# Top-32 attention with a gated mixer: the mask's biases made on ScalarE, and another order of the folds

## The chip, the cores and the metric

The kernel runs on one core of one Trainium2 chip. The metric is the device time of one execution in microseconds (us). Before the change the median of three runs is 985.09 us (983.68 to 985.43). The engines are named as the profile names them: PE is TensorE (matmuls), PEld its weight loads, DVE is VectorE, ACT is ScalarE, POOL is GpSimd, SP issues the DMAs.

## The reference

Three blocks follow one another, in float32, on batch 4, 8 heads, sequence 576, head width 64 (model width 512):

```
scores = q @ k.T / 8                       # per batch and head, 576 x 576
kth    = 32nd largest score of each row
attn   = softmax(where(scores >= kth, scores, -1e9)) @ v
x      = concat of the heads               # 4 x 576 x 512
gate   = sigmoid(causal 5-tap convolution of x along the sequence)
x      = (gate * (x @ w_val)) @ w_out
u      = x + token mixing (576 -> 256, relu, 256 -> 576)
out    = u + relu(u @ w_ch1) @ w_ch2       # 512 -> 1536 -> 512
```

## The kernel before

**Tiling.** Attention is cut into 80 units: 16 pairs of heads, each with four units of two 128-row tiles (one per head, `w = 2`) and a fifth of one tile that holds the last 64 rows of both heads (`w = 1`). A batch has 20 units. When a batch's units are done, its gate, its projections and its mixing follow: matmuls into the PSUM tiles `mo`, most of them as three products of split operands (L527 to L529).

**One unit** (`attn`). PE multiplies q with the left 288 columns of k into the PSUM tile `Sp` (L318), ACT copies them to `S` in SBUF (L324; L340 for `w = 1`), PE overwrites `Sp` with the right 288 columns, and ACT copies these to `S` too. Before its search for the 32 largest, DVE folds the row (`fold`, L412): left and right halves are compared element by element, the left half read from `S` and the right one straight from `Sp`. There are five folds. Called here by the names that the trace gives their outputs, they are: `A` (larger of the first quarters), `Sp` (larger of the second quarters, written beside the scores into columns 288 to 431 of the PSUM tile `Sp`), `y<-S,Sp` (all smaller ones), `X<-A,Sp` and `y<-A,Sp` (larger and smaller of the first two results). `topk` and `top32` then take eight at a time with MAX8 (L425 to L427, L442) and MATCH_REPLACE8 (L444), into `top`, 32 sorted values a row.

**The mask.** L346 makes two numbers per row in `nb`: the largest score times -0.125 and the 32nd times 2^100. It is one DVE instruction. Its two factors stand in the last two columns (1022 and 1023) of the PSUM tile `PT`, written once in `setup`. ACT makes `W` = relu(2^100 x (32nd - score)) with the second number as bias (L358), POOL subtracts `W` from `S` into `E` (L360), and ACT takes the exponential with the first number as bias (L363).

**Products with v.** PE transposes `E` into columns 0 to 639 of `PT` (L372), ACT copies them to `pT` (L377), PE multiplies with v into columns 640 to 767 of `PT` (L385 to L389), and ACT copies the result out (L393).

**What sets the order.** The kernel collects all operations with an engine, a cost, and keys that they read and write (class `Order`), places them by list scheduling with those costs, and issues them in order of planned start. Each engine then works through its list in order. The keys serve the planning only: the waits on semaphores are added afterwards from the tiles that the instructions touch, and accesses of two engines to the same PSUM bank come to wait for each other. For the planning, `fold` reads the key `Sp` in the first three folds alone, and the second copy of `Sp` writes that key, so it is placed behind these three. L346 has no key of `PT`.

**Buffers.** `S` has four, `top` and `nb` three, `E`, `W` and `pT` two each; `Sp` and `PT` have one each, of two PSUM banks.

Of the kernel before, what the change touches and what calls it, by code (L numbers as in the profile page):

```python
# [11 lines left out]
AF = mybir.ActivationFunctionType  # L12
OP = mybir.AluOpType
# [4 lines left out]
BIG = 2.0 ** 100  # L18
# [147 lines left out]
class Builder:  # L166
# [56 lines left out]
    def setup(self):  # L223
        nc = self.nc
        jp = self.tf[0][:, 0:128].bitcast(I32)
        nc.gpsimd.iota(jp, pattern=[[1, 128]], base=0, channel_multiplier=-1)
        nc.vector.tensor_scalar(self.ident, jp, 0.0, None, op0=OP.is_equal)
        z = self.tf[1][:, 0:64]
        nc.vector.memset(z, 0.0)
        for i in range(4):  # L230
            nc.vector.tensor_copy(self.rhl[:, i], z)
        for i in range(4):
            nc.vector.memset(self.xf[i][:, 0:4], 0.0)
        for i in range(self.nE):
            nc.vector.memset(self.Et[i][:, S:640], 0.0)
        nc.vector.memset(self.bad, 0.0)
        nc.vector.memset(self.PT[:, 1022:1023], -0.125)
        nc.vector.memset(self.PT[:, 1023:1024], BIG)


    def pe(self, c, f, r, w, late=0.0, part=1.0):
# [55 lines left out]
    def attn(self, p, u):  # L297

        nc = self.nc
        b, c = divmod(p, 4)  # L300
        i = self.cnt["unit"]
        self.cnt["unit"] += 1
        s = self.slot[p]
        w = 2 if u < 4 else 1
        St, kS = self.St[i % self.nS], [("S", i % self.nS, t) for t in range(w)]
        q, k = self.qk2[s][:, 0], self.qk2[s][:, 1]
        R = [("qk", s, 0), ("qk", s, 1)]
        Sp = self.Sp
        m, kM = self.top[i % 3], [("m", i % 3, t) for t in range(w)]
        if u < 4:  # L310

            for n in range(2):
                c0 = 288 * n

                def qk(c0=c0):
                    for t in range(2):
                        r = slice(64 * t, 64 * t + 64)
                        nc.tensor.matmul(Sp[:, t, 0:288], q[r, 128 * u:128 * u + 128], k[r, c0:c0 + 288],  # L318
                                         start=True, stop=True)

                self.pe(0.686, qk, R, ["Sp"])
                if n and self.fast:
                    self.fold(i, w, St, Sp[:, :, 0:288], kS)
                self.act(S, lambda c0=c0: nc.scalar.activation(St[:, :, c0:c0 + 288], Sp[:, :, 0:288], AF.Copy),  # L324
                         ["Sp"], [(x, n) for x in kS] + ["Sp"] * n)
        else:

            def qk():
                for c0, c1 in ((0, 288), (288, 512), (512, 576)):
                    n, s0 = divmod(c0, 288)  # L330
                    if c1 < S:
                        e = 288 if n == 0 else S
                        nc.tensor.matmul(Sp[0:64, n, 0:288], q[0:64, 512:S], k[0:64, c0:e], start=True, stop=True)
                    y = (c0 + 64) % S
                    nc.tensor.matmul(Sp[64:128, n, s0:s0 + c1 - c0], q[64:128, 512:S], k[64:128, y:y + c1 - c0],
                                     start=True, stop=True)

            self.pe(1.125, qk, R, ["Sp"])
            for n in range(2):
                self.act(288, lambda n=n: nc.scalar.activation(St[:, 0, 288 * n:288 * n + 288], Sp[:, n, 0:288], AF.Copy),  # L340
                         ["Sp"], [(kS[0], n)] + ["Sp"] * n)
                if n == 0 and self.fast:
                    self.fold(i, w, St, Sp[:, 1:2, 0:288], kS)
        nb, kN = self.nb[i % 3], ("nb", i % 3)
        (self.topk if self.fast else self.topk_any)(i, w, St, m, kS, kM)
        self.dve(2 * w, lambda: nc.vector.tensor_tensor(  # L346
            nb[:, 0:w], m[:, 0:w, 0:32:31], self.PT[:, 1022:1024].unsqueeze(1).to_broadcast([128, w, 2]), op=OP.mult), kM, [kN])
        vt = self.vt[s]
        o = self.PT[:, 640:768]
        pts = []  # L350
        E2, kE2 = self.Et[i % self.nE], [("E", i % self.nE, t) for t in range(2)]
        for t in range(w):
            j = self.cnt["tile"]
            self.cnt["tile"] += 1
            x, kx = St[:, t], [(kS[t], 0), (kS[t], 1)]
            E, W = E2[:, t * S:(t + 1) * S], self.Wt[j % self.nW]
            kE, kW = kE2[t], ("W", j % self.nW)
            self.act(S, lambda W=W, x=x, t=t: nc.scalar.activation(W, x, AF.Relu, bias=nb[:, t, 1:2], scale=-BIG),  # L358
                     kx + [kN], [kW], True)
            self.pool(S, lambda W=W, x=x, E=E: nc.gpsimd.tensor_tensor(E, x, W, op=OP.subtract),  # L360
                      kx + [kW], [kE])
            d = self.den[b % 2][:, c, 2 * u + t:2 * u + t + 1]
            self.act(S + 110, lambda E=E, d=d, t=t: nc.scalar.activation(  # L363
                E, E, AF.Exp, bias=nb[:, t, 0:1], scale=0.125, accum_out=d),
                [kE, kN], [kE, ("den", b % 2, c, 2 * u + t)], True)

            pT, kP = self.pT[j % self.nP], ("pT", j % self.nP)
            z = [0, 1, 2, 3, 4] if w == 1 else [5, 6, 7, 8, 4] if t else [0, 1, 2, 3]

            def tr(z=z):  # L370
                for y, k in enumerate(z):
                    nc.tensor.transpose(self.PT[:, y * 128:(y + 1) * 128], E2[:, k * 128:(k + 1) * 128], self.ident)  # L372

            n = 128 * len(z)
            kp = ["PT", "o"][:1 + (n > 512)]
            self.pe(0.109 * len(z) - 0.081, tr, kE2[0:1] if w == 2 and t == 0 else kE2, kp, 0.1)
            self.act(n, lambda pT=pT, n=n: nc.scalar.activation(pT[:, 0:n], self.PT[:, 0:n], AF.Copy), kp, [kP])  # L377
            pts.append((pT, kP))
        a, e = pts[0][0], pts[-1][0]
        n = 128 if w == 2 else 64  # L380
        g = 128 - n

        def pv():
            for y in range(4):
                nc.tensor.matmul(o[0:64, 0:n], vt[:, y], a[:, y * 128:y * 128 + n], start=(y == 0), stop=False)  # L385
                nc.tensor.matmul(o[64:128, 0:n], vt[:, 5 + y], e[:, y * 128 + g:y * 128 + 128], start=(y == 0), stop=False)
            r = slice(64, 128) if w == 2 else slice(0, 64)
            nc.tensor.matmul(o[0:64, 0:n], vt[0:64, 4], e[0:64, 512:512 + n], start=False, stop=True)
            nc.tensor.matmul(o[64:128, 0:n], vt[r, 4 if w == 2 else 9], e[r, 512 + g:640], start=False, stop=True)  # L389

        self.pe(1.39 if w == 2 else 0.877, pv, [x[1] for x in pts] + [("v", s)],
                ["o"], 0.1, 0.88)
        self.act(n, lambda: nc.scalar.activation(self.xf[c][:, 4 + 128 * u:4 + 128 * u + n], o[:, 0:n], AF.Copy),  # L393
                 ["o"], [("x", c, u)])

    def fold(self, i, w, St, right, kS):

        v = self.nc.vector  # L400
        kx = [(x, 0) for x in kS]
        A, Bm = self.At[:, 0:w], self.yt[:, 1].rearrange("p (t k) -> p t k", t=2)[:, 0:w]
        Ar = self.Sp[:, 0:w, 288:432]
        A1, A2 = self.Xt[i % 2][:, 0:w, 0:144], self.yt[:, 0].rearrange("p (t k) -> p t k", t=2)[:, 0:w, 0:144]
        kA, kB, kX = ([(n, t) for t in range(w)] for n in ("A", "B", ("X", i % 2)))
        l = St[:, 0:w, 0:288]
        kl, kr = kx + ["Sp"], ["Al", "Ar"]
        for o, ko, a, b, ka, f in ((A, ["Al"], l[:, :, 0:144], right[:, :, 0:144], kl, OP.max),
                                   (Ar, ["Ar"], l[:, :, 144:288], right[:, :, 144:288], kl, OP.max),
                                   (Bm, kB, l, right, kl, OP.min),  # L410
                                   (A1, kX, A, Ar, kr, OP.max), (A2, kA, A, Ar, kr, OP.min)):
            self.dve(w * a.shape[-1], lambda o=o, a=a, b=b, f=f: v.tensor_tensor(o, a, b, op=f), ka, ko)  # L412

# [381 lines left out]
```

## Time and profile before

| what | value |
|---|---|
| median of three runs | 985.09 us |
| the profiled execution, its own time | 985.71 us |
| its span, first to last instruction | 983.9 us |
| mean granted TensorE clock | 0.951 |
| PE, DVE, ACT, POOL busy | 870.9, 768.2, 554.1, 422.7 us |

The span leaves 1.8 us of the execution's own time outside it. Busy time is the union of an engine's instructions. An idle time is given with what ended it. Since each engine works in the order of its list, an instruction that waits holds up all that stands behind it.

### The profile page before, as it was taken

How to read it: one execution, taken by the hardware profiler on the slowest of the kernel's cores; microseconds unless marked ns; L12 is line 12 of the kernel's file. 1: busy time of each engine (PE TensorE's matmuls, PEld its weight loads, DVE VectorE, ACT ScalarE, POOL GpSimd, SP SyncE). 2: the span in 40 equal slices, each digit the busy share in tenths (PEclk: the TensorE clock that was granted, in tenths of full speed). 3: DMA queues.
4: the chain of work that ended last, by engine and by line, in shares of the span. 5: the costliest groups of instructions: out<-in, count | busy, mean ns of one | idle time of the engine just before them, and what ended most of it. 6: DMA issues, size and time to landing. Idle time of an engine off the chain costs nothing.

```text
span 983.9 us, 18581 instructions
## 1 busy us (share of the span) xinstructions
PE 870.9 (89%) x6585; PEld 714.7 (73%) x6585; DVE 768.2 (78%) x2735; ACT 554.1 (56%) x1095; POOL 422.7 (43%) x395
## 2 busy tenths in 40 slices
PE   3479587899898998889999999999999999989996
PEld 1246354588687777667787888778788889878996
DVE  8998988989899998999689769896997866912222
ACT  4476766767675757666676545477676543522100
POOL 2344445778686877754253222354343121412000
PEclk9767869999999999999999999999999999999998
DMA  3101104334245454542112334433032235231442
GB/s 108 36 14 54 36 27 142 126 128 175 78 132 179 154 173 156 173 164 82 62 47 100 129 102 151 138 103 108 15 102 87 86 120 182 91 107 65 156 166 95
DMA packets 33734, 106.96 MB, mean 109 GB/s; under 512 B 3872, under 2 KB 4128, under 8 KB 33632
## 3 DMA queue, kind: packets, MB, share of 16 engines
q1 hardware_dynamic: 33632, 105.68, 32.2%
q8 instruction: 54, 0.88, 0.4%
q14 instruction: 48, 0.39, 0.1%
HBM read 84.17 MB, written 21.50 MB: 107 GB/s over the span
## 4 chain that ended last, share of the span: by engine, by line
PE 50%; DVE 31%; ACT 12%; issue 4%; POOL 1%; DMA 0%; DVEq 0%; ACTq 0%; SPq 0%
PE mo L527 10%; PE mo L528 9%; PE mo L529 9%; PE Sp L318 6%; PE PT L372 5%; PE PT L385 5%; DVE top L442 5%; DVE Z L444 4%; DVE y L412 4%; ACT S L324 3%; DVE f L614 3%; DVE X L425 2%; ACT W L358 2%; ACT pT L377 2%; ACT E L363 2%
## 5 line engine op out<-in xcount | busy, mean ns | idle before, releaser
L527 PE MATMUL mo<-r,ring 128*128 128x288 f32 x1024 | 317.2, 310 | 6.0 <-DVE xf L594 2.0
L528 PE MATMUL mo<-r,ring 128*128 128x288 f32 x1024 | 303.1, 296 | 2.7 <-DVE r L477 1.9
L529 PE MATMUL mo<-r,ring 128*128 128x288 f32 x1024 | 302.7, 296 | 1.0 <-POOL ring L462 0.9
L360 POOL TENSOR_TENSOR E<-S,W 128x576 f32<-128x576 f32 x144 | 207.0, 1450 | 94.1 <-ACT W L358 78.8
L527 PEld LDWEIGHTS mo<-r,ring 128*128 128x128 f32 x1024 | 192.9, 188 | 31.7 <-issue 19.2
L528 PEld LDWEIGHTS mo<-r,ring 128*128 128x128 f32 x1024 | 193.1, 189 | 4.6 <-DVE r L477 3.0
L529 PEld LDWEIGHTS mo<-r,ring 128*128 128x128 f32 x1024 | 192.9, 188 | 1.7 <-POOL ring L462 1.7
L358 ACT ACTIVATE W<-S,nb 128x576 f32<-128x576 f32 x144 | 107.0, 770 | 77.8 <-DVE nb L346 77.1
L318 PE MATMUL Sp<-qk 64*128 64x288 f32 x512 | 111.7, 513 | 40.8 <-ACT S L324 17.6
L442 DVE MAX8 top<-Z 128x8 f32<-128x168 f32 x432 | 125.9, 323 | 0.7
L363 ACT ACTIVATE E<-E,nb 128x576 f32<-128x576 f32 x144 | 111.3, 773 | 24.9 <-POOL E L360 24.1
L372 PE MATMUL PT<-ident,E 128*128 128x128 f32 x656 | 107.4, 294 | 19.0 <-ACT pT L377 7.3
L377 ACT ACTIVATE pT<-PT 128x512 f32<-128x512 f32 (+1 forms) x144 | 94.2, 654 | 49.1 <-PE PT L372 48.3
L324 ACT ACTIVATE S<-Sp 128x576 f32<-128x576 f32 x128 | 83.2, 650 | 66.0 <-PE Sp L318 31.3
L431 POOL TENSOR_TENSOR bad<-X,top 128x6 f32<-128x6 f32 (+1 forms) x80 | 18.5, 231 | 224.6 <-DVE top L442 182.4
L372 PEld LDWEIGHTS PT<-ident,E 128*128 128x128 f32 x656 | 78.0, 148 | 48.1 <-ACT pT L377 14.6
L385 PE MATMUL PT<-pT,v 128*64 128x128 f32 (+1 forms) x640 | 86.6, 282 | 16.2 <-ACT pT L377 11.0
L318 PEld LDWEIGHTS Sp<-qk 64*128 64x128 f32 x512 | 44.7, 208 | 71.5 <-ACT S L324 29.9
L468 ACT ACTIVATE r<-mo 128x576 fp32r<-128x576 f32 (+2 forms) x76 | 47.3, 629 | 85.2 <-PE mo L529 80.7
L385 PEld LDWEIGHTS PT<-pT,v 128*64 128x64 f32 x640 | 67.8, 145 | 37.1 <-ACT pT L377 20.4
L636 DVE TENSOR_TENSOR f<-mo,f 128x576 f32<-128x576 f32 x64 | 47.9, 748 | 55.1 <-PE mo L529 55.1
L444 DVE MATCH_REPLACE8 Z<-top,Z 128x168 f32<-128x168 f32 x288 | 89.7, 317 | 0.0
(106 smaller groups left out, 1609.5 us busy)
## 6 DMA issues: line engine op xcount, KB each, us to landing
ring<-ch1d SPq DMA_DIRECT2D x36, 512.0 KB, 3.3
ring<-ch2d SPq DMA_DIRECT2D x36, 512.0 KB, 3.3
stage<-in_w_ch_dram SPq DMA_DIRECT2D x24, 512.0 KB, 3.6
qk<-in_qk_dram SPq DMA_DIRECT2D x32, 288.0 KB, 3.1
ch1d<-ring SPq DMA_DIRECT2D x12, 512.0 KB, 2.9
ch2d<-ring SPq DMA_DIRECT2D x12, 512.0 KB, 3.6
ring<-vald SPq DMA_DIRECT2D x12, 512.0 KB, 3.5
ring<-outd SPq DMA_DIRECT2D x12, 512.0 KB, 3.4
```

The source lines that it names most:

```text
L318: nc.tensor.matmul(Sp[:, t, 0:288], q[r, 128 * u:128 * u + 128], k[r, c0:c0 + 288], start=True, stop=True)
L358: self.act(S, lambda W=W, x=x, t=t: nc.scalar.activation(W, x, AF.Relu, bias=nb[:, t, 1:2], scale=-BIG), kx + [kN], [kW], True)
L360: self.pool(S, lambda W=W, x=x, E=E: nc.gpsimd.tensor_tensor(E, x, W, op=OP.subtract), kx + [kW], [kE])
L363: self.act(S + 110, lambda E=E, d=d, t=t: nc.scalar.activation(E, E, AF.Exp, bias=nb[:, t, 0:1], scale=0.125, accum_out=d), [kE, kN], [kE, ...
L372: nc.tensor.transpose(self.PT[:, y * 128:(y + 1) * 128], E2[:, k * 128:(k + 1) * 128], self.ident)
L377: self.act(n, lambda pT=pT, n=n: nc.scalar.activation(pT[:, 0:n], self.PT[:, 0:n], AF.Copy), kp, [kP])
L385: nc.tensor.matmul(o[0:64, 0:n], vt[:, y], a[:, y * 128:y * 128 + n], start=(y == 0), stop=False)
L442: self.dve(n, lambda src=src, o=o: v.max(o, src), k, [(kM, q)] + [kM] * (q in (0, 3)))
L444: self.repl(n, lambda src=src, o=o: v.match_replace(out=z, in_to_replace=o, in_values=src, imm_value=NEG), k + [(kM, q)], [kz])
L527: nc.tensor.matmul(o, wh, xh, start=(x == 0), stop=False)
L528: nc.tensor.matmul(o, wh, xl, start=False, stop=False)
L529: nc.tensor.matmul(o, wl, xh, start=False, stop=(x == last))
```

## The change

The DVE instruction of L346 goes, and with it the two constants in `PT`. Two ACT instructions take its place, one for each number, with the factor as an immediate; both read `top` and write `nb` in SBUF. `W` is placed behind the second, the exponential behind the first.

In `fold` the third fold (`y<-S,Sp`) moves ahead of the second (`Sp`), which for the planning now also depends on it; and the last two folds read the key `Sp`, so that the copy of the right half is placed behind all five.

```diff
-        nc.vector.memset(self.PT[:, 1022:1023], -0.125)
-        nc.vector.memset(self.PT[:, 1023:1024], BIG)
...
-        self.dve(2 * w, lambda: nc.vector.tensor_tensor(
-            nb[:, 0:w], m[:, 0:w, 0:32:31], self.PT[:, 1022:1024].unsqueeze(1).to_broadcast([128, w, 2]), op=OP.mult), kM, [kN])
+        for x, (z, f) in enumerate(((0, -0.125), (31, BIG))):
+            self.act(2 * w, lambda x=x, z=z, f=f: nc.scalar.activation(nb[:, 0:w, x], m[:, 0:w, z], AF.Copy, scale=f),
+                     kM, [(kN, x)])
...
-                     kx + [kN], [kW], True)
+                     kx + [(kN, 1)], [kW], True)
...
-                [kE, kN], [kE, ("den", b % 2, c, 2 * u + t)], True)
+                [kE, (kN, 0)], [kE, ("den", b % 2, c, 2 * u + t)], True)
...
-        kl, kr = kx + ["Sp"], ["Al", "Ar"]
+        kl, kr = kx + ["Sp"], ["Al", "Ar", "Sp"]
         for o, ko, a, b, ka, f in ((A, ["Al"], l[:, :, 0:144], right[:, :, 0:144], kl, OP.max),
-                                   (Ar, ["Ar"], l[:, :, 144:288], right[:, :, 144:288], kl, OP.max),
                                    (Bm, kB, l, right, kl, OP.min),
+                                   (Ar, ["Ar"], l[:, :, 144:288], right[:, :, 144:288], kl + kB, OP.max),
                                    (A1, kX, A, Ar, kr, OP.max), (A2, kA, A, Ar, kr, OP.min)):
```

The planner places everything anew. On DVE, a unit's folds in the second pair of heads stood like this before (numbers behind names tell buffers apart; `waits` names the engines that the row waits for):

```order
L412 TENSOR_TENSOR A<-S_71,Sp 128x288 [waits PE_49,Activation_49]
L346 TENSOR_TENSOR nb_84<-top_81,PT 128x4 [waits DVE_49,Activation_49]
L412 TENSOR_TENSOR Sp<-S_71,Sp 128x2x144 [waits DVE_49]
L412 TENSOR_TENSOR y<-S_71,Sp 128x576 [waits DVE_49]
L412 TENSOR_TENSOR X_75<-A,Sp 128x2x144
L412 TENSOR_TENSOR y<-A,Sp 128x2x144 [waits Activation_49]
L425 MAX X_75<-y 128x8 [waits DVE_49,Pool_49]
```

The same unit now, on DVE (the lines of the changed kernel are one or two lower; L496 is a weight conversion that the planner put between):

```order
L411 TENSOR_TENSOR A<-S_71,Sp 128x288 [waits PE_49,Activation_49]
L411 TENSOR_TENSOR y<-S_71,Sp 128x576
L496 TENSOR_SCALAR wa_106<-stage_63 128x512 [waits DMAHW4_49,Pool_49]
L411 TENSOR_TENSOR Sp<-S_71,Sp 128x2x144 [waits DVE_49]
L424 MAX X_75<-y 128x8
L411 TENSOR_TENSOR X_75<-A,Sp 128x2x144 [waits DVE_49]
L411 TENSOR_TENSOR y<-A,Sp 128x2x144
```

`nb` has left DVE's list, one wait on DVE's own results has gone from the first three folds, a MAX8 stands between the third and the fourth, and none of the last two folds waits for ACT.

On ACT, the stretch from one `Sp` copy to the next around the mask of another unit stood like this before:

```order
L324 ACTIVATE S_71<-Sp 128x2x288 [waits DVE_49,PE_49]
L358 ACTIVATE W_88<-S_70,nb_84 128x576 [waits Activation_49]
L358 ACTIVATE W_87<-S_70,nb_84 128x576 [waits Activation_49]
L393 ACTIVATE xf_162<-PT 128x128 [waits PE_49]
L324 ACTIVATE S_72<-Sp 128x2x288 [waits DVE_49,PE_49]
```

The mask of the same unit now, on ACT (L460 are splits of other data, L392 is the copy out of `PT`):

```order
L322 ACTIVATE S_71<-Sp 128x2x288 [waits PE_49]
L460 ACTIVATE ring_166<-wa_106 128x512 [waits Pool_49]
L345 ACTIVATE nb_84<-top_81 128x2 [waits DVE_49]
L345 ACTIVATE nb_84<-top_81 128x2
L460 ACTIVATE rhl<-rcp 128x9 [waits DVE_49]
L357 ACTIVATE W_88<-S_70,nb_84 128x576 [waits Activation_49]
L392 ACTIVATE xf_162<-PT 128x128 [waits PE_49]
```

The two new instructions stand ahead of `W`; the first waits for DVE, and `W` waits for ACT's own result.

## Rows read from the trace of the kernel before

**Rows 1.** The page: busy time of each engine, share of span, instructions.
```profile
PE 870.9 (89%) x6585; PEld 714.7 (73%) x6585; DVE 768.2 (78%) x2735; ACT 554.1 (56%) x1095; POOL 422.7 (43%) x395
```

**Rows 2.** Stretches, us: length, each engine's busy time (instructions), clock, DMA, GB/s.
```profile
0.00:194.00 194.00, 133.51 (x849) 83.28 (x850) 171.25 (x720) 125.20 (x263) 87.95 (x99) 0.80 0.21 68
194.00:450.00 256.00, 232.08 (x1819) 192.03 (x1818) 233.42 (x796) 168.31 (x329) 185.50 (x157) 0.99 0.43 147
450.00:850.00 400.00, 385.00 (x3080) 325.61 (x3077) 325.40 (x1172) 238.07 (x469) 137.00 (x133) 1.00 0.31 101
850.00:984.00 134.00, 120.29 (x845) 113.80 (x843) 38.13 (x52) 22.52 (x35) 12.22 (x8) 0.97 0.36 120
```

**Rows 3.** DVE timeline, 98 to 118 us: start, length, instruction [idle before, ended by].
```profile
98.46 0.44 DVE L412 TENSOR_TENSOR A<-S,Sp 128x288 f32<-128x288 f32 x1
99.35 0.16 DVE L346 TENSOR_TENSOR nb<-top,PT 128x4 f32<-128x4 f32 x1 [0.45 <-ACT pT L377]
99.42 0.46 DVE L412 TENSOR_TENSOR Sp<-S,Sp 128x288 f32<-128x288 f32 x1
99.91 0.75 DVE L412 TENSOR_TENSOR y<-S,Sp 128x576 f32<-128x576 f32 x1
100.59 0.45 DVE L412 TENSOR_TENSOR X<-A,Sp 128x288 f32<-128x288 f32 x1
100.95 0.45 DVE L412 TENSOR_TENSOR y<-A,Sp 128x288 f32<-128x288 f32 x1
...
106.27 0.44 DVE L412 TENSOR_TENSOR A<-S,Sp 128x288 f32<-128x288 f32 x1
...
107.92 0.45 DVE L412 TENSOR_TENSOR X<-A,Sp 128x288 f32<-128x288 f32 x1
109.08 0.45 DVE L412 TENSOR_TENSOR y<-A,Sp 128x288 f32<-128x288 f32 x1 [0.72 <-ACT S L324]
...
114.61 0.45 DVE L412 TENSOR_TENSOR A<-S,Sp 128x288 f32<-128x288 f32 x1
```

**Rows 4.** Timeline of all engines, 199 to 200 us.
```profile
199.10 0.27 PE L389 MATMUL PT<-pT,v 64*64 64x128 f32 x1
...
199.47 0.16 DVE L346 TENSOR_TENSOR nb<-top,PT 128x4 f32<-128x4 f32 x1 [2.31 <-PE PT L389]
...
199.67 0.78 ACT L358 ACTIVATE W<-S,nb 128x576 f32<-128x576 f32 x1 [2.15 <-DVE nb L346]
```

**Rows 5.** DVE's L346 in 0:194, 194:450, 450:850: count | busy, mean ns | idle before.
```profile
L346 DVE TENSOR_TENSOR nb<-top,PT 128x4 f32<-128x4 f32 (+1 forms) x21 | 3.1, 154 | 11.6 <-PE PT L389 4.8 <-PE PT L372 3.5 <-ACT pT L377 1.9
...
L346 DVE TENSOR_TENSOR nb<-top,PT 128x4 f32<-128x4 f32 (+1 forms) x23 | 3.5, 153 | 11.1 <-PE PT L389 6.7 <-PE PT L372 2.4 <-issue 1.3
...
L346 DVE TENSOR_TENSOR nb<-top,PT 128x4 f32<-128x4 f32 (+1 forms) x36 | 5.5, 152 | 6.9 <-PE PT L389 5.1 <-ACT pT L377 1.1 <-PE PT L372 0.2
```

**Rows 6.** DVE's last folds: 0:194, then 194:450 (two), then 450:850.
```profile
L412 DVE TENSOR_TENSOR y<-A,Sp 128x288 f32<-128x288 f32 (+1 forms) x22 | 9.3, 423 | 5.9 <-ACT S L324 5.0 <-ACT S L340 1.0
...
L412 DVE TENSOR_TENSOR y<-A,Sp 128x288 f32<-128x288 f32 (+1 forms) x22 | 9.3, 421 | 4.2 <-ACT S L324 3.7 <-ACT S L340 0.5
L412 DVE TENSOR_TENSOR X<-A,Sp 128x288 f32<-128x288 f32 (+1 forms) x22 | 9.2, 419 | 2.4 <-ACT S L324 2.1 <-ACT S L340 0.2
...
L412 DVE TENSOR_TENSOR y<-A,Sp 128x288 f32<-128x288 f32 (+1 forms) x36 | 15.0, 418 | 10.9 <-ACT S L324 8.7 <-ACT S L340 1.4 <-PE Sp L318 0.6
```

**Rows 7.** ACT timeline, 72.5 to 75 us: a small copy and what follows.
```profile
72.65 0.20 ACT L461 ACTIVATE rhl<-rcp 128x9 fp32r<-128x9 f32 x1
72.75 0.58 ACT L377 ACTIVATE pT<-PT 128x512 f32<-128x512 f32 x1
```

**Rows 8.** In 0:194: ACT's copy of Sp, and DVE's first fold.
```profile
L324 ACT ACTIVATE S<-Sp 128x576 f32<-128x576 f32 x37 | 24.0, 650 | 24.6 <-PE Sp L318 9.1 <-DVE X L412 7.9 <-DVE y L412 6.5
...
L412 DVE TENSOR_TENSOR A<-S,Sp 128x288 f32<-128x288 f32 (+1 forms) x22 | 9.1, 412 | 1.0 <-ACT diag L601 1.0
```

**Rows 9.** PE's products with v in 0:194.
```profile
L385 PE MATMUL PT<-pT,v 128*64 128x128 f32 (+1 forms) x160 | 25.9, 318 | 12.9 <-ACT pT L377 8.2 <-DVE nb L346 4.6
```

**Rows 10.** Line L527's weight loads: ns min/median/max, first and last start us.
```profile
L527 PEld LDWEIGHTS mo<-r,ring x1024: 186/188/330, 193.8 to 974.8; 128*128 128x128 f32 x171
```

## The prediction

> **What bounds the kernel now.** The page's busy times come first: PE 870.9 us and DVE 768.2 us of a span of 983.9, ACT 56% [rows 1]. A mean like this mixes stages, so the second view is the busy time by stretches, cut where the mixer's matmuls begin (193.8 us [rows 10]) and where attention has ended. It shows four stages [rows 2]. From 0 to 194 us there is attention alone: DVE is busy 171.3 of 194 us (88%), PE 133.5, and PE's granted clock averages 0.80, between its levels of 1.2 and 2.4 GHz. From 194 to 450 DVE (233.4 of 256) and PE (232.1) are both at 91%. From 450 to 850 PE is at 96% (385.0 of 400) and DVE at 81%. From 850 on PE does the last batch's mixing nearly alone. So DVE sets the pace first, both share it next, then PE.
>
> The third view is DVE's timeline in the first stage. From one unit's first fold to the next it takes 7.81 us (98.46 to 106.27) and 8.34 us (106.27 to 114.61), and between them the list is dense but for two holes: `nb` waited 0.45 us for an ACT copy out of `PT`, and a last fold waited 0.72 us for ACT's copy of `Sp` [rows 3]. Neither hole is arithmetic: the fold and the copy both only read `Sp`, and `nb` reads two columns that nobody writes. A larger hole of this kind is at 199 us: the last matmul into `PT` ends at 199.37, `nb` starts at 199.47 after 2.31 us of waiting, and `W` on ACT follows at 199.67 [rows 4]. The fourth view, the groups by line, gives the holes their sum in each stage [rows 5, 6].
>
> **The change part by part.** The sums are made against the profiled execution, 985.71 us, of which 983.9 are its span; the median is 0.6 us lower.
>
> *Removal of `nb` from DVE.* It is busy 3.1, 3.5 and 5.5 us in the three stages at some 0.153 us each [rows 5], but neighbours overlap: the next fold starts 0.07 us after it [rows 3]. I take 0.1 us, between 0.07 and 0.15: 21, 23 and 36 instructions give 2.1, 2.3 and 3.6 us.
>
> *Its waits.* 11.6, 11.1 and 6.9 us of DVE idle [rows 5] go, since the new instructions touch only SBUF. PE waited for `nb` too, 4.6 us in its products with v in the first stage alone [rows 9], and that goes with them.
>
> *The fold's waits for the copy.* 5.9 us in the first stage, 4.2 + 2.4 = 6.6 in the second, 10.9 in the third (0.6 of these for PE) [rows 6]. In the new order the copy comes behind all folds, so none of them can wait for it.
>
> *The new order of folds.* Two folds that don't depend on each other start 0.36 us apart (100.59, 100.95); a fold that waits for the write before it starts 0.49 after it (99.42, 99.91) [rows 3]. Before, two of the first three folds wait so, now one. That is 0.13 us per unit: 2.7, 3.0 and 4.7 us. Between zero (another wait takes its place) and twice that, I take it once. The MAX8 put ahead of the fourth fold covers that one's wait: it takes the 0.36 us or so that the write needs.
>
> *The two instructions on ACT.* No row shows them. The nearest is a copy of 9 columns: 0.20 us, and the next instruction begins 0.10 us after it starts [rows 7]. As `W` waits for the second of them, a pair holds ACT between 0.20 us (two issues) and 0.40 us (both in full); I take 0.10 + 0.20 = 0.30. In the first stage that is 21 x 0.30 = 6.3 us on an engine with 194 - 125.2 = 68.8 us free [rows 2], so its busy time is hidden; what isn't hidden is the way from the last `top` to `W`, 0.1 to 0.2 us longer than the 0.20 from the start of `nb` to `W` [rows 4]. Four buffers of `S` lie behind that way, and I cost it at nothing. If that cover is gone, it costs up to 44 x 0.30 = 13.2 us before 450 us.
>
> *The later copy.* It now waits for the fifth fold. Before, ACT's copy already waited for a `y` or an `X` fold (6.5 and 7.9 us in the first stage), so much of the delay is there today [rows 8]. At most the copy moves by two folds of 0.36 us. While `Sp` is refilled, DVE has the unit's whole search ahead (106.27 to 114.61 less the folds, over 5 us [rows 3]); that hides it. DVE's first fold waited 1.0 us in the stage, for something else [rows 8].
>
> *The sum.* First stage: instruction and fold order give 2.1 + 2.7 = 4.8 us in full, as DVE sets the pace; the waits of 11.6 + 5.9 = 17.5 us I count by half, 8.8, because what a hole absorbs today (a late `Sp`, a late `S`) will partly be waited for elsewhere. That is 13.6. Second stage: 2.3 + 3.0 + 11.1 + 6.6 = 23.0, PE's own idle time of 23.9 us allows it, but PE is as full as DVE, so a third: 7.7. Third stage: PE's 15.0 us of idle time cap everything; I take 1, since DVE is not what PE waits for there. Last stage: nothing. 985.7 - 13.6 - 7.7 - 1 = 963.4, less the 0.6 of the median 962.8; I give 963 us. With only the instructions and the order counted in the first stage, and half of them in the second, the sum ends at 985.7 - 4.8 - 2.7 = 978; with all of the first two stages at 985.7 - 22.3 - 22 = 941.
>
> **The rivals.**
>
> *Everything comes through.* The holes close and nothing takes their place in the first two stages: about 941 to 950, 945 in the middle. For it: the dense units of 7.8 to 8.3 us, in which DVE never waits for data except at these two places. Against it: PE would have to run from 194 to 450 us without any hole.
>
> *The waits move.* The copy now always comes last, `Sp` is refilled later, and DVE waits at its first fold what it doesn't wait at its last: only instructions and fold order are left, 978 us (973 to 983). For it: PE's clock is low in the first stage, so a refill is slow. Against it: the 5 us of search.
>
> *Nothing arrives.* The gain of the first stage is spent in the second, where the newly placed list meets a full PE: 985 us, within the bound below.
>
> *Slower.* The pair stands at the head of ACT's list and waits for DVE's `top`; behind it stand the copies of `Sp` and `PT`, which DVE and PE wait for. Before, `nb` waited on DVE, and `W` alone waited on ACT. If each of the 44 pairs before 450 us holds the copies up by its full 0.30 us and the holes saved on DVE come back as waits for `S` and `Sp`, the sum is 985.7 + 13.2 = 999 us. It decides once DVE's waits at the first fold exceed the 17.5 us saved in the first stage, from 1.0 now. For it: the list of ACT, where a split and a copy out of `PT` now stand among pair and `W`. Against it: ACT's 68.8 us free. The Trainium skill ("ScalarE: Activation LUTs", Rules for kernel authors) speaks for this rival: it sends multiplications to VectorE rather than ScalarE. Going by that page's 186 ns + 0.833 ns per element for an instruction with immediates, a pair would be an estimated 0.38 us against DVE's one of 0.153, and the 999 would become about 1002; the trace's 0.20 us for 9 columns agrees with that price [rows 7], and whether the rule holds here is a matter of which engine sets the pace.
>
> **How the numbers follow.** Forecast 0.50 (own range 952 to 973), everything through 0.13, waits move 0.18, nothing arrives 0.07, slower 0.12. A measurement of this kernel can tell about 0.2%, 2 us, from no change. Faster is 0.50 + 0.13 + 0.18 = 0.81, the same 0.07, slower 0.12. The range of 943 to 986 leaves out the slower case and some 0.05 of the lowest.
>
> **What would show it.** Right: `nb` absent from DVE; the last folds without idle time before them; a first stage so much shorter that the first L527 matmul comes near 180 us instead of 193.8; a DVE share over 91% in the first stage; ACT's pair at 0.2 us an instruction and no growth of the wait of PE for ACT's copies. Wrong: the first fold's idle time up by several us in the first stage (the waits moved), ACT's copies starting later after their data is there (slower), or the first stage shorter by 10 us with the total unmoved (nothing arrives).

## The result, and the profile after

The changed kernel takes 953.55 us in the median of four runs (951.91 to 954.19). Against runs of the kernel before on the same chip the ratio is 0.967, with a 95% interval of 0.963 to 0.970; measured once more on another chip it is 0.970 (0.967 to 0.973). That is 3.0 to 3.3% less; the forecast was 963, with a range of 943 to 986. The profiled execution took 951.91 us, of which 950.0 are its span. Ratios here are of undisturbed runs alone.

The page of the changed kernel, busy time of each engine (against [rows 1]):

```profile
PE 859.5 (90%) x6585; PEld 710.5 (75%) x6585; DVE 764.7 (80%) x2653; ACT 572.5 (60%) x1255; POOL 426.9 (45%) x395
```

DVE has 82 instructions fewer (80 `nb` and two constants), ACT 160 more. PE does the same 6585 matmuls in 11.4 us less; the stretches below put 10.5 of these into the first stage, where its granted clock has risen (11 of its matmuls also lie in another stretch now). The mixer's first matmuls, in the changed kernel (against [rows 10]):

```profile
L526 PEld LDWEIGHTS mo<-r,ring x1024: 186/188/330, 178.4 to 940.9; 128*128 128x128 f32 x171
```

So the first stage ends 15.4 us earlier. To compare the rest, both spans are cut at the same three events: the first of these matmuls, the issue of batch 0's last output, and that of batch 2's. The outputs, issued by SP, first before, then after:

```profile
423.80 0.38 SPq L710 DMA_DIRECT2D out_dram<-f  x1
...
835.14 0.34 SPq L710 DMA_DIRECT2D out_dram<-f  x1
```

```profile
385.53 0.42 SPq L709 DMA_DIRECT2D out_dram<-f  x1
...
801.11 0.34 SPq L709 DMA_DIRECT2D out_dram<-f  x1
```

Busy times in the stretches between these events (columns as in [rows 2]), before:

```profile
0.00:193.80 193.80, 133.31 (x848) 83.08 (x848) 171.05 (x718) 125.13 (x263) 87.75 (x99) 0.80 0.21 67
193.80:423.80 230.00, 210.09 (x1644) 173.77 (x1642) 208.98 (x730) 151.98 (x299) 175.47 (x148) 0.99 0.45 152
423.80:835.10 411.30, 393.65 (x3142) 332.74 (x3144) 338.18 (x1227) 246.29 (x482) 140.69 (x137) 1.00 0.31 102
835.10:984.00 148.90, 133.83 (x958) 125.13 (x954) 49.98 (x62) 30.69 (x52) 18.75 (x12) 0.96 0.35 114
```

And after:

```profile
0.00:178.40 178.40, 122.81 (x837) 77.61 (x837) 166.65 (x679) 124.69 (x294) 89.10 (x97) 0.89 0.24 80
178.40:385.50 207.10, 198.44 (x1561) 167.39 (x1561) 195.01 (x643) 147.40 (x318) 170.23 (x142) 1.00 0.47 162
385.50:801.10 415.60, 405.37 (x3242) 341.56 (x3237) 353.05 (x1271) 269.70 (x593) 148.81 (x145) 0.99 0.32 102
801.10:950.00 148.90, 132.83 (x958) 123.97 (x954) 49.98 (x62) 30.69 (x52) 18.73 (x12) 0.97 0.34 114
```

In the first stretch DVE's idle time falls from 193.8 - 171.1 = 22.7 to 178.4 - 166.7 = 11.7 us, and its busy time by 4.4: that is the 15.4. The work in the two first stretches isn't quite the same: the shorter one holds the folds of 21 units instead of 22 and the search of 38 tiles instead of 40, and in exchange more weight conversions (L496, L499 and L501, 24.6 us against 18.3 before). The second stretch is 22.9 us shorter. But PE did 83 matmuls less in it, 11.7 us, and these turn up in the third: what the second really gained is PE's idle time, from 19.9 to 8.7, 11.2 us. In the third PE's idle time falls from 17.7 to 10.2, 7.4 us, although the stretch with its added work is 4.3 longer. The last doesn't move. 15.4 + 11.2 + 7.4 = 34.0, against 33.9 for the span.

DVE's folds in the first stretch of the changed kernel (against [rows 6, 8]):

```profile
L411 DVE TENSOR_TENSOR y<-S,Sp 128x576 f32<-128x576 f32 (+1 forms) x21 | 14.3, 680 | 2.4 <-PE Sp L316 2.3
L411 DVE TENSOR_TENSOR Sp<-S,Sp 128x288 f32<-128x288 f32 (+1 forms) x21 | 9.0, 428 | 0.4
L411 DVE TENSOR_TENSOR A<-S,Sp 128x288 f32<-128x288 f32 (+1 forms) x21 | 8.8, 417 | 2.8 <-PE Sp L316 2.8
L411 DVE TENSOR_TENSOR y<-A,Sp 128x288 f32<-128x288 f32 (+1 forms) x21 | 8.7, 416 | 0.0
L411 DVE TENSOR_TENSOR X<-A,Sp 128x288 f32<-128x288 f32 (+1 forms) x21 | 8.5, 407 | 0.0
```

The last folds no longer wait. Whichever fold comes first (`A` in some units, `y<-S,Sp` in others) now waits for PE's refill of `Sp`, 5.1 us in all, against 1.0 for `A` before, which was a wait for ACT.

The mask in the changed kernel, ACT and DVE from 102.4 to 104 us (against [rows 3, 4]), and a second pair on ACT:

```profile
102.48 0.30 ACT L345 ACTIVATE nb<-top 128x2 f32<-128x2 f32 x2 [1.64 <-DVE top L441]
102.48 0.69 DVE L411 TENSOR_TENSOR y<-S,Sp 128x576 f32<-128x576 f32 x1
...
102.68 0.20 ACT L460 ACTIVATE rhl<-rcp 128x9 fp32r<-128x9 f32 x1
102.78 0.76 ACT L357 ACTIVATE W<-S,nb 128x576 f32<-128x576 f32 x1
103.09 0.44 DVE L411 TENSOR_TENSOR A<-S,Sp 128x288 f32<-128x288 f32 x1
...
103.56 0.46 DVE L411 TENSOR_TENSOR Sp<-S,Sp 128x288 f32<-128x288 f32 x1
...
103.94 0.46 DVE L424 MAX8 X<-y 128x8 f32<-128x288 f32 x1
```

```profile
74.78 0.29 ACT L345 ACTIVATE nb<-top 128x2 f32<-128x2 f32 x2
75.01 0.78 ACT L357 ACTIVATE W<-S,nb 128x576 f32<-128x576 f32 x1
```

The pair keeps ACT busy for 0.30 us. In the first place a small instruction for other data (`rhl`) stands between it and `W`; in the second `W` follows directly and starts 0.23 us after the pair does. DVE goes on with its folds beside it.

### The profile page after: what moved, and what is told of

It reads as the page before. It is cut to its first block, busy times and chain, and to the rows that moved or that the text cites. A ratio compares the mean times of both kernels' runs of the same rounds, so it can differ in the third digit from the quotient of the medians.

```text
span 950.0 us, 18427 instructions
## 1 busy us (share of the span) xinstructions
PE 859.5 (90%) x6585; PEld 710.5 (75%) x6585; DVE 764.7 (80%) x2653; ACT 572.5 (60%) x1255; POOL 426.9 (45%) x395
## 4 chain that ended last, share of the span: by engine, by line
PE 62%; DVE 25%; ACT 7%; POOL 2%; issue 2%; DMA 2%; SPq 0%; DVEq 0%; ACTq 0%; POOLq 0%
PE mo L526 14%; PE mo L527 13%; PE mo L528 13%; PE Sp L316 6%; PE PT L371 5%; PE PT L384 4%; DVE top L441 4%; DVE Z L443 4%; DVE y L411 3%; DVE f L613 2%; DVE X L424 2%; PE PT L387 2%; PE mo L605 2%; DVE wa L501 1%; ACT r L467 1%
## 5 line engine op out<-in xcount | busy, mean ns | idle before, releaser
L527 PE MATMUL mo<-r,ring 128*128 128x288 f32 x1024 | 303.0, 296 | 2.8 <-POOL r L461 2.2
L526 PEld LDWEIGHTS mo<-r,ring 128*128 128x128 f32 x1024 | 192.9, 188 | 32.6 <-issue 19.9
L527 PEld LDWEIGHTS mo<-r,ring 128*128 128x128 f32 x1024 | 193.1, 189 | 4.8 <-POOL r L461 3.4
L316 PE MATMUL Sp<-qk 64*128 64x288 f32 x512 | 106.3, 493 | 25.8 <-ACT S L322 18.3
L371 PE MATMUL PT<-ident,E 128*128 128x128 f32 x656 | 105.1, 290 | 23.8 <-ACT E L362 13.4
L430 POOL TENSOR_TENSOR bad<-X,top 128x6 f32<-128x6 f32 (+1 forms) x80 | 20.9, 261 | 230.5 <-DVE top L441 224.0
L371 PEld LDWEIGHTS PT<-ident,E 128*128 128x128 f32 x656 | 77.5, 146 | 50.2 <-ACT E L362 19.9
L384 PE MATMUL PT<-pT,v 128*64 128x128 f32 (+1 forms) x640 | 87.3, 284 | 9.2 <-ACT pT L376 9.1
L385 PE MATMUL PT<-pT,v 128*64 128x128 f32 (+1 forms) x640 | 87.4, 284 | 0.0
```

What stands on the lines that cost most here:

```text
L526: nc.tensor.matmul(o, wh, xh, start=(x == 0), stop=False)
L527: nc.tensor.matmul(o, wh, xl, start=False, stop=False)
```

## The experiments

Theories: **waits**, that VectorE's holes at `nb` and at the folds set the pace and that closing them is the gain; against it that only one half of the change does anything, that `nb` had to leave VectorE, or that the new **plan** as such is what helps. The table gives the ratio to the kernel before with its 95% interval, the ratio times 985.3 us (the absolute medians come from several chips), and two events of the one profiled execution: first L527-type matmul, and batch 0's last output.

| kernel | ratio | interval | us | mixer begins | batch 0 out |
|---|---|---|---|---|---|
| before | 1 | | 985.3 | 193.8 | 423.8 |
| changed | 0.967 | 0.963 to 0.970 | 952.6 | 178.4 | 385.5 |
| e1, biases on ScalarE alone | 0.974 | 0.971 to 0.977 | 959.8 | 178.5 | 393.2 |
| e2, folds and copy alone | 0.974 | 0.971 to 0.977 | 959.7 | 184.9 | 403.6 |
| e3, constants in SBUF | 0.984 | 0.981 to 0.988 | 969.7 | 185.3 | 413.1 |
| e4, e3 with the folds of e2 | 0.962 | 0.957 to 0.967 | 947.8 | 178.6 | 400.6 |
| e5, order of folds alone | 1.005 | 1.002 to 1.008 | 990.2 | 204.9 | 429.5 |
| e6, copy last alone | 0.981 | 0.976 to 0.986 | 966.7 | 189.8 | 409.6 |
| e7, pair twice | 0.958 | 0.954 to 0.962 | 943.6 | 176.0 | 390.0 |
| e8, `nb` on GpSimd | 0.961 | 0.957 to 0.964 | 946.4 | 183.3 | 400.9 |
| e9, pair twice, plan of the changed | 0.974 | 0.971 to 0.977 | 959.3 | 185.4 | 393.2 |
| e10, pair once, plan of e7 | 0.959 | 0.955 to 0.963 | 945.1 | 177.7 | 390.8 |
| e11, 12 planner rounds instead of 4 | 0.972 | 0.969 to 0.975 | 957.5 | 180.2 | 390.4 |
| e12, changed, again | 0.970 | 0.967 to 0.973 | 955.7 | 177.2 | 383.4 |

**e1 and e2: each half by itself.** e1 has the hunks of the diff that concern `nb`, e2 the one in `fold`; no other line differs.

> Only the first half of the change: nb by two ScalarE operations, folds as before. Theory 1 (VectorE's holes set the pace, and each half of the change closes its own holes): of the working before the run the nb part is 2.1 + 5.8 us in the first stage and about a third of 13.4 in the second, some 12.4; the whole change moved 32 us where 23 were worked out, so scaled by 1.4 about 17 us, 968 us (962 to 974), with the last folds still idle by some 20 us in all. Theory 2 (the gain is the folds' and the new plan's, the nb part only pays for two more ScalarE operations): 980 to 990. Theory 3 (a lucky new plan of the whole): anything, and the two halves don't add.

> Only the second half: the new order of folds and the copy behind them, nb on VectorE with its constants in PT. Theory 1: 2.7 + 3.0 us in the first stage and a third of 9.6 in the second, some 8.9, scaled by 1.4 about 12 us: 973 us (966 to 978); nb's idle time stays at 25 to 30 us in all and the last folds' is gone. Theory 2: 955 to 962, nearly all of the gain. Rival on the other side (the later copy only moves the waits): 983 to 988.

Both halves work, and both give 2.6%, more than the waits theory had for either. Together they give 3.0 to 3.3% and not 5.2. Either the holes stand in for one another, or the three new plans differ for other reasons; e3 and e4 bear on that. In e2 the last two folds' idle time is 0.0 us, as forecast, and that of `nb` 22.0, less than forecast. e2's time lies in the range that the theory of the folds alone gave. The folds over the whole span, before and in e1:

```profile
L412 DVE TENSOR_TENSOR y<-A,Sp 128x288 f32<-128x288 f32 (+1 forms) x80 | 33.6, 420 | 21.0 <-ACT S L324 17.4 <-ACT S L340 2.9 <-PE Sp L318 0.6
L412 DVE TENSOR_TENSOR X<-A,Sp 128x288 f32<-128x288 f32 (+1 forms) x80 | 33.4, 417 | 4.4 <-ACT S L324 3.3 <-PE Sp L318 0.8 <-ACT S L340 0.2
L412 DVE TENSOR_TENSOR A<-S,Sp 128x288 f32<-128x288 f32 (+1 forms) x80 | 32.9, 411 | 6.3 <-PE Sp L318 4.0 <-ACT diag L601 1.0 <-ACT f L616 0.7
```

```profile
L411 DVE TENSOR_TENSOR y<-A,Sp 128x288 f32<-128x288 f32 (+1 forms) x80 | 33.7, 421 | 32.2 <-ACT S L322 27.9 <-ACT S L338 2.4 <-PE Sp L316 1.8
L411 DVE TENSOR_TENSOR X<-A,Sp 128x288 f32<-128x288 f32 (+1 forms) x80 | 33.3, 417 | 3.1 <-ACT S L322 2.8 <-ACT S L338 0.3
L411 DVE TENSOR_TENSOR A<-S,Sp 128x288 f32<-128x288 f32 (+1 forms) x80 | 32.9, 411 | 20.5 <-PE Sp L316 16.1 <-ACT pT L376 2.1 <-ACT diag L600 1.0
```

With `nb` gone and everything planned anew the last two folds wait 35.3 us, against 25.4 before, and the first one 20.5, against 6.3. The theory that only the folds matter falls, since e1 alone gives as much; that the new plan as a whole does it is still open here, since halves that don't add were its sign.

**e3: the waits alone, in the same plan.**

```diff
-        nc.vector.memset(self.PT[:, 1022:1023], -0.125)
-        nc.vector.memset(self.PT[:, 1023:1024], BIG)
+        nc.vector.memset(self.kc[:, 0:1], -0.125)
+        nc.vector.memset(self.kc[:, 1:2], BIG)
...
-            ... self.PT[:, 1022:1024].unsqueeze(1).to_broadcast([128, w, 2]), op=OP.mult), kM, [kN])
+            ... self.kc.unsqueeze(1).to_broadcast([128, w, 2]), op=OP.mult), kM, [kN])
```

> The kernel before with one thing changed: nb's two constants stand in an SBUF tile instead of PT. The planner sees the same costs and keys, so every engine's list is the same as before; nb stays on VectorE, only its waits for PE and ScalarE at the PT banks go. Theory 1 (waits): 29.6 us of idle time before nb gone, half of 11.6 and a third of 11.1 through, 9.5, scaled by 1.4 about 13 us: 972 us (966 to 978). Theory 3 (the plan): 985, since the plan is the same. A third possibility, that it is the instruction's leaving VectorE that counts: 983 to 985.

Each engine's list is as before, and the kernel is 1.6% faster, 15.6 us where 13 were expected. That settles that the waits at `PT` cost time by themselves: neither the plan nor the instruction changed, only where its operand stands. `nb` and the folds in e3, whole span (groups), and one instance of `nb` with POOL beside it (timeline):

```profile
L347 DVE TENSOR_TENSOR nb<-top,kc 128x4 f32<-128x4 f32 (+1 forms) x80 | 27.1, 340 | 0.1
...
L413 DVE TENSOR_TENSOR y<-A,Sp 128x288 f32<-128x288 f32 (+1 forms) x80 | 33.6, 420 | 21.7 <-ACT S L325 17.5 <-ACT S L341 3.6 <-PE Sp L319 0.6
L413 DVE TENSOR_TENSOR X<-A,Sp 128x288 f32<-128x288 f32 (+1 forms) x80 | 33.3, 417 | 5.2 <-ACT S L325 4.2 <-PE Sp L319 0.8 <-ACT S L341 0.2
L413 DVE TENSOR_TENSOR A<-S,Sp 128x288 f32<-128x288 f32 (+1 forms) x80 | 32.8, 410 | 7.8 <-PE Sp L319 5.0 <-ACT pT L378 0.8 <-ACT diag L602 0.8
```

```profile
61.97 1.40 POOL L361 TENSOR_TENSOR E<-S,W 128x576 f32<-128x576 f32 x1
62.15 1.24 DVE L347 TENSOR_TENSOR nb<-top,kc 128x4 f32<-128x4 f32 x1
```

The idle time of 29.6 us is gone (0.1), but an instruction now takes 0.340 us in the mean instead of 0.153: this one ends at 63.39, just after POOL's subtraction at 63.37. So the constants in `PT` had bought something, too. And with the plan held, the folds hardly take the wait over: these three groups wait 34.7 us instead of 31.7. What e1's folds wait more is thus not simply `nb`'s wait at another place; it came only where everything was planned anew.

**e4: the waits at `PT` and the folds, `nb` still on VectorE** (the edits of e3 and e2 together).

> The new folds, and nb as one VectorE instruction with its constants in SBUF. Theory 1: close to the changed kernel, 2 to 6 us slower for 80 small instructions of 0.1 us on VectorE: 955 to 960 us. If moving nb off VectorE is what the bias half is worth: 965 to 975, near the folds alone. If the two ScalarE operations cost something: faster than the changed kernel, 945 to 953.

0.962, with an interval that overlaps the changed kernel's: `nb` needn't leave VectorE for the gain. Every engine's list in e4 is that of e2, so this is a second case in which only `nb`'s operand moved:

```profile
L346 DVE TENSOR_TENSOR nb<-top,PT 128x4 f32<-128x4 f32 (+1 forms) x80 | 11.8, 153 | 22.0 <-PE PT L389 6.5 <-PE PT L372 5.7 <-ACT pT L377 5.6
```

```profile
L347 DVE TENSOR_TENSOR nb<-top,kc 128x4 f32<-128x4 f32 (+1 forms) x80 | 20.8, 265 | 0.2
```

From e2 (first line) to e4 the ratio falls from 0.974 to 0.962, with the intervals apart, and all five folds together wait 29.2 us instead of 25.4. The two parts nearly add here: 1.6% (e3) and 2.6% (e2) alone, 3.8% together. So that e1 and e2 add up to more than the changed kernel gives doesn't show that one wait stands in for the other. The time lies in the range given to a ScalarE pair that costs something (945 to 953), but e4 has another plan than the changed kernel, and e10 below is as fast with the pair.

**e5 and e6: the second half taken apart.** e5 leaves out the key, e6 the order:

```diff
e5, against e2:
-        kl, kr = kx + ["Sp"], ["Al", "Ar", "Sp"]
+        kl, kr = kx + ["Sp"], ["Al", "Ar"]
e6, against the kernel before:
-        kl, kr = kx + ["Sp"], ["Al", "Ar"]
+        kl, kr = kx + ["Sp"], ["Al", "Ar", "Sp"]
```

> The kernel before with only the folds' order changed: the third fold ahead of the second, which depends on it; the last two folds don't read the key of Sp, so the copy may be planned between them as before. The folds alone (order and copy) gave a ratio of 0.974, 25 us. Theory 1a (a hole is worth what it is wide): one wait on VectorE's own write less, 0.13 us for each of 80 units, 10 us at most and 7 to 8 of it through: 977 (973 to 981), with the last folds still idle for ScalarE's copy by 20 us or more. Theory 1b (the copy behind the folds is what counts): 983 to 986. Theory 1c (the order is what counts): 960 to 968.

> The kernel before with only the last two folds' key of Sp: the copy comes behind all five folds, whose order stays. Theory 1a: some 15 to 17 us, 969 (964 to 974), the last folds' idle time gone and the first fold's up by half of it. Theory 1b (the copy alone counts): 958 to 964. Theory 1c (the order alone counts, the copy only moves its wait to the first fold): 982 to 990.

e6 is as the waits theory had it in time, though its first folds now wait 27.7 us, about what the last ones did (1.7 of them up to 190 us). e5 misses all its expectations: with the order alone the kernel is 0.5% slower. The folds of e5 in 0 to 205 us, its first stage:

```profile
L412 DVE TENSOR_TENSOR A<-S,Sp 128x288 f32<-128x288 f32 (+1 forms) x22 | 9.3, 425 | 0.0
L412 DVE TENSOR_TENSOR X<-A,Sp 128x288 f32<-128x288 f32 (+1 forms) x22 | 9.2, 419 | 6.4 <-ACT S L324 5.6 <-PE Sp L318 0.8
L412 DVE TENSOR_TENSOR y<-A,Sp 128x288 f32<-128x288 f32 (+1 forms) x21 | 8.9, 422 | 9.2 <-ACT S L324 5.6 <-PE Sp L318 3.6
```

Planned without the key, the copy and even the next unit's matmuls come between more of the last folds: they wait 15.6 us in the first stage instead of 6.7 (5.9 [rows 6] and 0.8 at `X<-A,Sp`), and the stage is 11 us longer, at a granted clock of 0.76 instead of 0.80. Whether the order loses this by itself, or the new plan does, no run tells apart. e2, which has the order and the key, is 0.7% below e6, but the intervals overlap a little and the plans differ, so the order's own gain isn't shown either. In e6 `nb` waits more than before, in 0 to 190 us:

```profile
L346 DVE TENSOR_TENSOR nb<-top,PT 128x4 f32<-128x4 f32 (+1 forms) x20 | 3.0, 156 | 17.8 <-PE PT L372 5.9 <-ACT xf L393 5.3 <-PE PT L389 4.4
```

That is 17.8 us against 11.6 before [rows 5], 6.2 us more. It may be the folds' wait at another place; since the plan is new, that isn't shown.

**e7: the pair twice.** Every entry of the pair is made twice, planned as four operations.

```diff
-        for x, (z, f) in enumerate(((0, -0.125), (31, BIG))):
-            self.act(...)
+        for _ in range(2):
+            for x, (z, f) in enumerate(((0, -0.125), (31, BIG))):
+                self.act(...)
```

> The changed kernel with the pair of ScalarE operations made twice (160 more of 0.2 us, the second pair writes the same values again). Theory 1 (ScalarE's work is hidden beside VectorE and then TensorE): 951 to 956, no more than 3 us above the changed kernel's ratio of 0.967. Rival (the pair is on the way that sets the end): 42 pairs of 0.3 us in the first two stages on that way, 965 to 970.

Neither: with 160 instructions more it is faster than the changed kernel, 0.958.

**e8: `nb` on GpSimd**, its constants in SBUF as in e3.

```diff
-            self.act(2 * w, ...)                       # twice
+        self.pool(2 * w, lambda: nc.gpsimd.tensor_tensor(
+            nb[:, 0:w], m[:, 0:w, 0:32:31], self.kc.unsqueeze(1).to_broadcast([128, w, 2]), op=OP.mult),
+                  kM, [(kN, 0), (kN, 1)])
```

> The changed kernel with nb made by one GpSimd operation (its two constants in SBUF) instead of two on ScalarE: neither VectorE nor ScalarE has the work. Theory 1 (VectorE's holes are what counts, and they are closed as well here): 948 to 957, like the changed kernel. If ScalarE's pair cost something: 943 to 950. If the way from top to W counts, since GpSimd's list is in order too and nb may stand behind a subtraction of 1.45 us: 957 to 970.

0.961: whichever engine does it, the time is about the same, as long as it isn't VectorE reading `PT`. The time lies in the range given to a ScalarE pair that costs something (943 to 950), but the plan differs as well, so what the engine itself is worth can't be read from it.

**e9 to e12: plan or instructions.** e9 issues each operation of the changed kernel twice inside one planned entry; e10 plans the four entries of e7 and issues the last two; e11 sets `ROUNDS = 12`; e12 is the changed kernel.

```diff
e9:
+            self.act(2 * w, lambda x=x, z=z, f=f: [nc.scalar.activation(...) for _ in range(2)], kM, [(kN, x)])
e10:
+        for y in range(2):
+            for x, (z, f) in enumerate(((0, -0.125), (31, BIG))):
+                self.act(2 * w, lambda x=x, z=z, f=f, y=y: y and nc.scalar.activation(...), kM, [(kN, x)])
```

> The changed kernel with each of the two ScalarE operations issued twice in a row, in the plan of the changed kernel (the planner does not see the second). With pairs doubled in a plan made for it the ratio was 0.958, below the 0.967 of the changed kernel. Theory P (that gain came from the plan, and 160 more ScalarE operations are hidden work): the ratio of the changed kernel or up to 0.004 above it, 0.967 to 0.971. Theory L (more ScalarE operations by themselves help, by spacing): 0.955 to 0.961. Theory A (ScalarE's pair is on the way): 0.975 to 0.985.

> The plan made for doubled pairs, with each pair issued once. Theory P (the plan): 0.955 to 0.960, like the doubled pairs in this plan. Theory L (the number of operations): 0.965 to 0.969, like the changed kernel.

> The changed kernel with 12 rounds of the planner instead of 4: the same instructions in a partly different order. It shows how far a new order alone moves the time. Theory P: within 0.955 to 0.972, not the same as the changed kernel. If the order matters little: the changed kernel's time within 2 us.

> The changed kernel itself, beside the other three on one chip: a ratio of 0.967 (0.963 to 0.970), by its first measurement. What the other three differ from it by is read against this run.

For what e7 gained, the plan it is. e7 and e10 have one plan, 160 instructions apart: 0.958 and 0.959. e9 and e12 have another: 0.974 and 0.970. Between the plans lies 1.1% (0.959 against 0.970, intervals apart), about 11 us. e11's, a third one, is 0.972, which isn't apart from e12. e9 lies just outside the ranges set from the first measurement; beside e12 it is 0.4% above, with intervals that overlap. In the first stage e9 and e12 differ more: e9's ends at 185.4, e12's at 177.2, in the same plan (one execution each; first e9, then e12):

```profile
0.00:185.40 185.40, 131.24 (x836) 82.41 (x836) 164.77 (x679) 131.79 (x333) 89.97 (x97) 0.83 0.23 77
```

```profile
0.00:177.20 177.20, 123.95 (x837) 78.05 (x837) 166.67 (x679) 124.54 (x294) 88.37 (x97) 0.87 0.24 80
```

e9's first folds up to 186 us:

```profile
L412 DVE TENSOR_TENSOR y<-S,Sp 128x576 f32<-128x576 f32 (+1 forms) x22 | 15.2, 693 | 9.1 <-PE Sp L316 6.2 <-ACT nb L345 1.4 <-ACT pT L377 0.8
```

Against 2.4 in the changed kernel's first stage and 0.6 in e12 up to 186 us. That is what the rival "slower" would look like: the pair holds up the copies behind it, `Sp` is refilled later, and the first fold waits. But PE's granted clock was lower too, 0.83 against 0.87, and the same matmuls took it 7.3 us longer; which of the two delayed the refill isn't shown. In the other plan the doubled pair's first stage ends at 176.0, the single pair's at 177.7. At the end of e9's and e12's executions 5.3 of the 8.2 us are left (954.0 against 948.7). e10, with 945.1 us in the median (938.69 to 948.76), is the fastest version that carries only the change's own instructions, 1.1% ahead of the changed kernel.

## Why the prediction was right, and by how much each step was off

*The bound.* Right. The first three stages gained in the order that was forecast, 15.4, 11.2 and 7.4 us, and the last didn't move. Of the signs, the first mixer matmul came at 178.4 us, DVE is busy for 93% of the first stage, and the last folds wait 0.0 us. A sign of the rival showed too: the first fold's idle time rose, by 4.1 us.

*First stage, forecast 13.6, measured 15.4.* Instructions and order: forecast 4.8, and DVE's busy time fell by 4.4. That the two agree is chance, since the stretch holds other work than before (above). Over the whole span, with the same work, busy time falls by 3.5 us only, where this term made 18.4 of all three stages: `nb`'s 12.1 us are gone, but the weight conversions take 83.3 us instead of 75.5, for a reason that no run shows. Waits: of 17.5 half was counted, 8.8; idle time fell by 11.0. It isn't half of each, however. `nb`'s 11.6 went whole; the folds had 6.7 at the last two, of which 4.1 came back at the first (5.1 against 1.0), and waits for weights' DMAs grew by 3.7 (4.5 against 0.8): 11.6 + 6.7 - 4.1 - 3.7 = 10.5, near the 11.0. e3, in the old plan, bears out the first of these: DVE's idle time up to the mixer falls by 11.0 us there too, its busy time rises by 2.4, and the stage is 8.5 shorter. For the folds the rival "the waits move" came true in part.

*Second stage, forecast 7.7, measured 11.2* by PE's idle time. A third of 23.0 was too little; half would have been right.

*Third stage, forecast 1, measured 7.4.* This is the worst term of the sum. PE's idle time was taken as not VectorE's doing, because PE was at 96%. But its holes closed too, from 17.7 to 10.2 us, even though VectorE's folds wait more there than before (25.2 us at `y<-S,Sp` and 8.4 at `A` in the changed kernel). The third stage of e3, in the old plan:

```profile
413.10:822.40 409.30, 394.31 (x3144) 335.64 (x3144) 340.98 (x1227) 245.82 (x482) 140.80 (x137) 0.99 0.31 103
```

PE's idle time is 15.0 us here: the waits at `PT` were 2.7 of the 7.4. Whether the folds' waits or the new plan did the rest, no run tells apart.

*The new order of folds, 0.13 us per unit.* The step holds where it was measured: three folds took 1.65 us from 106.27 to 107.92 before [rows 3] and 1.46 from 102.48 to 103.94 after, 0.19 less. As a gain of its own it isn't shown: e5 is slower than the kernel before, and e2 and e6 differ by less than two plans can.

*The pair, 0.30 us.* Exactly so as busy time (102.48 to 102.78), 23.9 us of ScalarE in all; where `W` follows directly it starts sooner, after 0.23 us (74.78 to 75.01). Whether "costed at nothing" was right for the first stage is open: e9's is 8.2 us longer than e12's, at a lower clock, while e7's is 1.7 shorter than e10's. At the end doubling the pair costs 0.4% or less, within what can be measured. The multiplications' move from VectorE to ScalarE, against which the prediction quoted the Trainium skill ("ScalarE: Activation LUTs", Rules for kernel authors), was beside the point here: the page weighs the two engines' speed per element. The 0.38 us that the prediction estimated for a pair from the page was too much, as the second instruction starts before the first ends. The trace shows that each 0.153 us on VectorE came with 0.37 us of waiting (29.6 us over 80) for where its operand stood.

*TensorE's clock.* It rose from 0.80 to 0.89 in the first stage, and PE's work there took 10.5 us less. It was busy 69% of the stage before and after (133.3 of 193.8, 122.8 of 178.4). That the stage got shorter because of the clock isn't excluded by any run, since no kernel changed the clock alone. e3 changed the waits alone and ends its stage at 185.3, but its clock rose with it, to 0.85. The first stages of e3 and e1:

```profile
0.00:185.30 185.30, 125.71 (x848) 78.56 (x848) 173.46 (x718) 124.55 (x263) 87.32 (x99) 0.85 0.22 70
```

```profile
0.00:178.50 178.50, 125.65 (x836) 78.30 (x836) 163.62 (x676) 127.07 (x298) 87.04 (x98) 0.85 0.23 74
```

At one clock, 0.85, the stage lasts 185.3 us in e3 and 178.5 in e1, and at 0.89 it lasts 178.4 in the changed kernel. So the clock alone doesn't set its length.

*What the forecast left out.* The plan. A list scheduler that places 18,000 instructions anew moves the time by itself: 1.1% between two plans of the same work here. That is a third of the whole gain, so the last per cent of the ratio says little about the two edits. What is shown with the plan held is the worth of the waits at `PT`: 1.6% in the old plan (e3), 1.2% in e2's (e4). The second half gave something each time it was added, but always with a new plan: 2.6% on the kernel before (e2), 2.2 on e3 (e4), 0.4 to 0.7 on e1 (the changed kernel), the last hardly clear of the intervals. Its own size stays open.

## What to carry to other kernels

Look at what ends the idle time of a small instruction on the engine that sets the pace: here 12 us of constants' arithmetic carried 30 us of waiting, because its operand shared a PSUM bank with other engines' work. Closing either half gave 2.6%, both 3.0 to 3.3%, but in one plan the waits at `PT` and the folds nearly added: try each half alone, and with the plan held where that can be done (e3, e4), before it is credited. And where a planner orders the work, compare an edit with edits that only change the plan, before a per cent is put down to it.

## What the runs showed of the hardware

A VectorE operation on 4 columns with both operands in SBUF took 1.24 us where the same with one operand in PSUM never took more than 0.163, and it ended with GpSimd's subtraction that had started 0.18 us before it (e3; 0.340 us in the mean over 80). 22 of the 80 took over 0.25 us there; 21 of these had started beside a running GpSimd instruction and ended 0.01 to 0.02 us after it. The Trainium skill ("SBUF — State Buffer", Who interferes with whom) has this: an instruction of VectorE with two inputs in SBUF contends with one of GpSimd that reads SBUF, the contended ports are an exclusive lock, and the order of issue decides which of the two blocks. The trace agrees. The kernel before paid for avoiding that with the waits at `PT`, 29.6 us against the 15.0 us (27.1 - 12.1) that the blocking adds in e3.
